# Linear attention and two feed-forward networks on one core: TensorE's order from the plan, later transfers in the plan, scalings on two engines

## The chip, the core and the metric

The kernel runs on one core of a Trainium2 chip, with TensorE (PE), VectorE (DVE), ScalarE (ACT), GpSimd (POOL) and the queue of SyncE (SP), each with its own list of instructions that it takes in order. The metric is the time of one execution on the device in us, the median of several.

## What is computed

```python
for t in range(S):                      # attention: B, H, S, D = 4, 8, 768, 64
    state = gamma * state + k[:, :, t] outer v[:, :, t]
    y[:, :, t] = scale * q[:, :, t] @ state
x = y as (3072 tokens, 512)
h = x @ w_in                            # first network, 512 -> 1024 -> 512
u = h * softmax(h)
x = ((u - mean(u)) / sqrt(var(u) + 1e-6) * g_ln) @ w_out
h = x @ w_in2                           # second network, 512 -> 2048 -> 512
out = (h * cos(h)) @ w_out2
```
(Shortened. q, k, v are float32; the weights come as 64-bit floating point numbers.)

## The kernel before

Attention runs over 24 steps: two pairs of batches, each in 12 chunks of 64 positions, all heads at once. A step loads q, k (twice: kt by dimension, kn by position) and v in six transfers, 1 MB in all. `scores` makes 16 small matmuls into bank sc, and VectorE multiplies them with the decay mask mg into X (`masks`); mg is made for each step by GpSimd from constants (`prep`), where ScalarE also scales the four parts of kn. `state` adds 16 matmuls into S, which ScalarE copies into the next step's W. `att_out` makes y, from which come xh and xl, a split of the float32 value into two parts.

Each matmul of the networks is done as three, with high and low parts (w1h, w1l and so on). In the first network `mm1` makes h of a step in bank hA (or hB for steps 1 and 3) in two halves c of 512 columns, each of 12 matmuls of 512 columns. `norm` makes u: VectorE's maximum, ScalarE's exp, VectorE's product, ScalarE's squares, GpSimd's power, and at last a scaling of u by ScalarE. Four steps make a block of 512 tokens: `transp` transposes u on TensorE into banks tr, ScalarE and VectorE make lt of it, `mm2` makes y, which ScalarE copies to ys and a transfer writes to y1d. The second network (`up`, `down`) begins when the attention is done.

The weights come in raw blocks of 512 KB. `convert` makes float32 of one: ScalarE reads the upper bits into a buffer top, VectorE joins them with the rest, and both make the high and the low part. First come eight blocks of w_in1 (tiles big, w1h, w1l), eight of w_out1 (o1h, o1l), then 32 of the second network (tiles raw), of which 28 are written back as float32 (kept) and read again later.

The order on all engines but TensorE is made at build time by `Plan.order`: each operation has an engine, an assumed duration, its dependencies and, for a transfer, an assumed landing time of LEAD + length + LAND after the issue. The plan takes the operation that can start first, at equal times the one with the longest chain behind it. TensorE's operations keep the order of the program:

```python
if at < len(pe) and need[pe[at]] == 0:
    c = [(max(free[e], ready_at[pe[at]]), pe[at])]
```
The plan's times reach the chip only as order; on the chip each instruction waits for what it needs, and all behind it on its engine wait too.

Of the kernel before, what the change touches and what calls it, by code (L numbers as in the profile page):

```python
# [24 lines left out]
C = 64  # L25
# [23 lines left out]
class Plan:  # L49
# [5 lines left out]

    SEM = 0.06
    LEAD = 1.2
    LAND = 0.6
    LANES = 8

    def __init__(self):
        self.ops = []
        self.chain = False
        self.last = []
        self.keys = []
        self.writers = {}
        self.readers = {}

    def add(self, eng, occ, fn, r=(), w=(), lat=None, port=False, xfer=0.0, after=()):
        n = len(self.ops)  # L70
        deps = {}
# [32 lines left out]
    def order(self):  # L104
# [30 lines left out]
        at = 0  # L135
# [3 lines left out]
        for i in range(n):  # L139
            if need[i] == 0 and ops[i][0] != "PE":  # L140
                pools[ops[i][0]].append(i)
        left = n
        out = []
        while left:
            best = None
            for e in free:
                if e == "PE":
                    if at < len(pe) and need[pe[at]] == 0:
                        c = [(max(free[e], ready_at[pe[at]]), pe[at])]
                    else:  # L150
                        continue
                else:
                    c = []
                    for i in pools[e]:
# [13 lines left out]
            eng, occ, fn, _, lat, prt, xfer = ops[i]  # L168
            if e == "PE":
                at += 1  # L170
            else:
                pools[e].remove(i)
# [22 lines left out]
def body(ctx: ExitStack, tc: tile.TileContext, qx, kt, kn, vn, c_sc, c_mg,  # L195
# [13 lines left out]
    mg = const.tile([128, 2, NHP, C], F32, name="mg")  # L209
    cs = const.tile([128, 3, NI, NHP], F32, name="cs")  # L210
# [38 lines left out]
    NRAW, NTOP, NWT, NA = 3, 3, 2, 3  # L249
# [20 lines left out]
    def dma(fn, size, r=(), w=(), occ=0.47, eng="SP", after=()):  # L270
# [23 lines left out]
    def load_step(n):  # L294
        bp, i = steps[n]
        s = n % NA
        X, W = a_X[s], a_W[s]
        q = qx[bp, i].rearrange("p (j s) -> p j s", s=C)
        v = vn[bp, i].rearrange("p (j s) -> p j s", s=D)
        dma(lambda: nc.sync.dma_start(out=a_kt[n % 2], in_=kt[bp, i].rearrange("p (j s) -> p j s", s=C)),  # L300
            (128, 2048), w=[("kt", n % 2)])
        dma(lambda: nc.sync.dma_start(out=X[64:128, 0], in_=q[64:128]), (64, 2048), w=[("X", s, "q", 0)], occ=0.6)
        dma(lambda: nc.sync.dma_start(out=X[0:64, 1], in_=q[0:64]), (64, 2048), w=[("X", s, "q", 1)], occ=0.6)
        dma(lambda: nc.sync.dma_start(out=a_kn[s], in_=kn[bp, i].rearrange("p (j s) -> p j s", s=2 * D)),
            (128, 2048), w=[("kn", s, a) for a in range(NHP)])
        dma(lambda: nc.sync.dma_start(out=W[0:64, 0], in_=v[0:64]), (64, 2048), w=[("W", s, "v", 0)], occ=0.6)
        dma(lambda: nc.sync.dma_start(out=W[64:128, 1], in_=v[64:128]), (64, 2048), w=[("W", s, "v", 1)], occ=0.6)
        if i == 0:
            for half, (r, par) in enumerate(((slice(64, 128), 0), (slice(0, 64), 1))):
                P.add("POOL", 0.55, lambda r=r, par=par: nc.gpsimd.memset(W[r, par], 0.0),  # L310
                      w=[("W", s, "st", half)])

    def prep(n):
# [5 lines left out]
        if i + 1 < NI:  # L319
            k = a_kn[n % NA]  # L320
            for a in range(NHP):
                act(k[:, a], k[:, a], AF.Copy, [("cs",)], [("kn", n % NA, a)], 0.295, scale=cs[:, 2, i, a:a + 1])

    def score_pair(n, j):
        k, X = a_kt[n % 2], a_X[n % NA]
        nc.tensor.matmul(out=p_sc[0:64, j], lhsT=k[64:128, j], rhs=X[64:128, 0, j], start=True, stop=True)  # L326
        nc.tensor.matmul(out=p_sc[64:128, j], lhsT=k[0:64, j], rhs=X[0:64, 1, j], start=True, stop=True)

    def state_pair(n, j):
# [3 lines left out]
        for r, par in HALF:  # L333
            nc.tensor.matmul(out=p_S[r, j], lhsT=k3[r, j], rhs=W[r, par, j],
# [595 lines left out]
```

## Time and profile before

| | us |
|---|---|
| three runs | 911.92, 914.95, 915.22 |
| profiled execution | 913.03 |
| span from its first to its last instruction | 911.3 |
| PE busy | 880.4 (97%) |
| VectorE, ScalarE, GpSimd busy | 547.6, 458.5, 45.3 |
| mean granted clock of TensorE | 0.989 |
| read and written in HBM | 64.29 and 19.92 MB, 92 GB/s over the span |

The span leaves out what lies ahead of the first and behind the last instruction. Busy shares are means over all stages. A time in a row of the timeline counts from the start of the span.

### The profile page before, as it was taken

Reading aid. Unit: us, or ns where it says so; the run is one execution under the profiler, and the core shown is the slowest. Engines: PE = TensorE matmul, PEld = TensorE weight load, DVE = VectorE, ACT = ScalarE, POOL = GpSimd, SP = SyncE. Lnnn points to the kernel's source line nnn. Section 1 sums busy time; section 2 is a strip of 40 time slices with the busy share of each in tenths; the row PEclk is TensorE's granted clock in tenths of the full one; section 3 lists DMA queues with packets and bytes.
Section 4 is the critical chain, followed back from the end, with each engine's and each line's share of the span. In section 5 each row is a group of like instructions: output and inputs, shape, how many; then the busy total and the mean of one; then the engine's idle time right before and its main releaser. Section 6 shows DMA issues by size and latency. Waiting matters only on the chain.

```text
span 911.3 us, 14625 instructions
## 1 busy us (share of the span) xinstructions
PE 880.4 (97%) x5888; PEld 725.2 (80%) x5888; DVE 547.6 (60%) x946; ACT 458.5 (50%) x768; POOL 45.3 (5%) x63
## 2 busy tenths in 40 slices
PE   5897998999999999999999999999999999999997
PEld 4686887787888878888888888888888888888886
DVE  4788756646255364746557566666665665566553
ACT  5789957766466464544334343434343443344332
POOL 2121210101011000000000000000000000000000
PEclk8998999999999999999999999999999999999999
DMA  9983599994231124130030003000200120011002
GB/s 313 286 273 93 182 295 325 299 334 148 74 105 59 47 72 149 70 116 1 1 92 1 1 1 92 1 1 24 70 0 1 45 49 1 0 30 40 1 0 47
DMA packets 38804, 85.17 MB, mean 93 GB/s; under 512 B 5456, under 2 KB 5584, under 8 KB 38736
## 3 DMA queue, kind: packets, MB, share of 16 engines
q1 hardware_dynamic: 37728, 81.80, 28.9%
q10 hardware_dynamic: 1008, 2.44, 0.8%
q8 instruction: 46, 0.75, 0.3%
q14 instruction: 22, 0.18, 0.1%
HBM read 64.29 MB, written 19.92 MB: 92 GB/s over the span
## 4 chain that ended last, share of the span: by engine, by line
PE 78%; DMA 11%; ACT 5%; DVE 4%; issue 1%; SPq 1%; POOL 0%; ACTq 0%; DVEq 0%
PE h L615 29%; PE acc L652 29%; PE hA L480 7%; PE y L546 7%; DMA raw<-w_in_dram 3%; DMA kn<-kn_dram 2%; PE tr L546 2%; DMA big<-w_in_dram 2%; PE tr L522 2%; ACT u L275 2%; DMA kept_out<-wt 1%; PE y L391 1%; ACT top L275 1%; PE sc L326 1%; DVE X L278 1%
## 5 line engine op out<-in xcount | busy, mean ns | idle before, releaser
L627 ACT ACTIVATE r<-r,hp 128x512 f32<-128x512 f32 x96 | 69.5, 724 | 146.2 <-DVE r L625 146.2
L546 PE MATMUL y<-lt,o1h 128*128 128x512 f32 x320 | 105.2, 397 | 1.3 <-ACT ys L551 1.3
L629 DVE TENSOR_TENSOR r<-r,h 128x512 f32<-128x512 f32 x96 | 66.0, 687 | 61.2 <-ACT r L627 61.2
L621 DVE SCALAR_TENSOR_TENSOR r<-ki,h 128x512 f32<-128x512 int32 x96 | 65.9, 686 | 55.3 <-ACT ki L619 55.3
L633 DVE TENSOR_TENSOR gl<-r,gh 128x512 fp32r<-128x512 f32 x96 | 66.3, 691 | 47.6 <-ACT gh L631 47.0
L652 PE MATMUL acc<-o2u,gh 128*128 128x512 f32 x288 | 94.5, 389 | 0.0
L619 ACT ACTIVATE ki<-h 128x512 int32<-128x512 f32 x96 | 57.4, 598 | 73.4 <-PE h L615 73.3
L652 PE MATMUL acc<-o2h,gh 128*128 128x512 f32 x240 | 93.4, 389 | 0.0
L652 PE MATMUL acc<-o2h,gl 128*128 128x512 f32 x240 | 93.4, 389 | 0.0
L652 PE MATMUL acc<-o2l,gh 128*128 128x512 f32 x240 | 93.4, 389 | 0.0
L631 ACT ACTIVATE gh<-r 128x512 fp32r<-128x512 f32 x96 | 60.7, 632 | 55.9 <-DVE r L629 55.9
L480 PE MATMUL hA<-w1h,xh 128*128 128x512 f32 x176 | 73.7, 419 | 3.8 <-DVE u L286 3.5
L615 PE MATMUL h<-yh,w1h 128*128 128x512 f32 x192 | 74.7, 389 | 0.0
L615 PE MATMUL h<-yh,w1l 128*128 128x512 f32 x192 | 74.7, 389 | 0.0
L615 PE MATMUL h<-yl,w1h 128*128 128x512 f32 x192 | 74.7, 389 | 0.0
L546 PEld LDWEIGHTS y<-lt,o1h 128*128 128x128 f32 x320 | 60.0, 188 | 15.3 <-ACT ys L551 1.8
L480 PE MATMUL hA<-w1h,xl 128*128 128x512 f32 x176 | 71.0, 404 | 0.0
L480 PE MATMUL hA<-w1l,xh 128*128 128x512 f32 x176 | 69.1, 398 | 0.0
L623 DVE SCALAR_TENSOR_TENSOR r<-ki,r 128x512 f32<-128x512 int32 x96 | 66.4, 692 | 3.2
L652 PEld LDWEIGHTS acc<-o2u,gh 128*128 128x128 f32 x288 | 54.1, 188 | 11.2
L546 PE MATMUL y<-lt,o1l 128*128 128x512 f32 x160 | 62.4, 390 | 0.0
L615 PE MATMUL h<-yh,w2a 128*128 128x512 f32 x192 | 59.5, 391 | 0.0
(105 smaller groups left out, 1704.8 us busy)
## 6 DMA issues: line engine op xcount, KB each, us to landing
raw<-w_in_dram SPq DMA_DIRECT2D x16, 511.8 KB, 5.9
raw<-w_out_dram SPq DMA_DIRECT2D x16, 511.8 KB, 5.4
kt<-kt_dram SPq DMA_DIRECT2D x24, 256.0 KB, 4.9
X<-qx_dram SPq DMA_DIRECT2D x48, 128.0 KB, 4.5
kn<-kn_dram SPq DMA_DIRECT2D x24, 256.0 KB, 4.7
W<-vn_dram SPq DMA_DIRECT2D x48, 128.0 KB, 4.1
y1d<-ys SPq DMA_DIRECT2D x24, 256.0 KB, 2.5
x<-y1d SPq DMA_DIRECT2D x24, 256.0 KB, 3.2
```

Source lines behind the costliest of these rows:

```text
L275: return P.add("ACT", occ, lambda: nc.scalar.activation(out=out, in_=in_, func=func, **kw), r, w, lat)
L480: nc.tensor.matmul(out=h, lhsT=a[:, k], rhs=w[:, k, s], start=(k + m == 0), stop=(k == KD - 1 and m == 2))
L546: nc.tensor.matmul(out=y1(), lhsT=w[:, j, ds], rhs=lts[j][:, a], start=(j + m == 0), stop=(j == K1 - 1 and m == 2))
L615: nc.tensor.matmul(out=p2["h2"][b], lhsT=w2tile(c, lo)[:, k, cs], rhs=p2[a][:, k], start=(k + m == 0), stop=(k == KD - 1 and m == 2))
L619: P.add("ACT", 0.5, lambda: nc.scalar.activation(out=p2["ki"][s], in_=p2["h2"][b], func=AF.Identity, scale=INV2PI, bias=0.25), [("h2", b)] ...
L621: P.add("DVE", 0.61, lambda: V.scalar_tensor_tensor(out=p2["r"][s], in0=p2["ki"][s], scalar=-C1, in1=p2["h2"][b], op0=ALU.mult, op1=ALU.ad ...
L623: P.add("DVE", 0.61, lambda: V.scalar_tensor_tensor(out=p2["r"][s], in0=p2["ki"][s], scalar=-C2, in1=p2["r"][s], op0=ALU.mult, op1=ALU.add ...
L627: P.add("ACT", 0.62, lambda: nc.scalar.activation(out=p2["r"][s], in_=p2["r"][s], func=AF.Sin, bias=hp[:, 0:1]), (), [("r", s)])
L629: P.add("DVE", 0.6, lambda: V.tensor_tensor(out=p2["r"][s], in0=p2["r"][s], in1=p2["h2"][b], op=ALU.mult), [("h2", b)], [("r", s)])
L631: P.add("ACT", 0.54, lambda: nc.scalar.activation(out=p2["gh"][g], in_=p2["r"][s], func=AF.Copy), [("r", s)], [("gh", g)])
L633: P.add("DVE", 0.6, lambda: V.tensor_tensor(out=p2["gl"][g], in0=p2["r"][s], in1=p2["gh"][g].bitcast(F32), op=ALU.subtract), [("r", s), (" ...
L652: nc.tensor.matmul(out=p2["acc"][t], lhsT=p2[a][g][:, ts_], rhs=o2tile(j, lo), start=(j == 0 and m == 0), stop=(j == K2 - 1 and m == 2))
```

## The change

`Plan.order` chooses among the next ten operations of TensorE's list: the one that can start first, where waiting for another engine costs 0.3 us more and each place in the list 0.05. A transfer is counted to land later (LAND 1.5 for 0.6, and 2.5 more for a raw weight from the ninth on, `bulk`), and a bulk transfer is placed only where the transfers ahead of it are at most 2.0 us from done. An operation may have a second form on another engine (`alt`): k's scaling and u's normalization go to ScalarE or VectorE, whichever ends first in the plan. q, k and v of a step lie in one tensor in HBM and in six slots of one tile, three tiles in turn (kt had two). The top buffers are two instead of three. The start is written anew: step 0 and the constants, now one transfer, ahead of the weights, and step 2 ahead of the last four blocks of w_in1; an exp of one column stands first on ScalarE.

```diff
-    LAND = 0.6
+    LAND = 1.5
     LANES = 8
+    BEHIND = 2.0
+    LATE = 2.5
+    WINDOW = 10
+    MARGIN = 0.3
+    STEP = 0.05
...
+        def begin(i, e):
+            occ, prt = (ops[i][1], ops[i][5]) if e == ops[i][0] else (self.alts[i][1], self.alts[i][3])
+            t = max(free[e], ready_at[i])
+            if prt and port[1] != e:
+                t = max(t, port[0])
+            if ops[i][6]:
+                t = max(t, lanes[-self.LANES])
+                if i in self.bulk:
+                    t = max(t, dma - self.BEHIND)
+            return t, occ
...
             for e in free:
                 if e == "PE":
-                    if at < len(pe) and need[pe[at]] == 0:
-                        c = [(max(free[e], ready_at[pe[at]]), pe[at])]
-                    else:
+                    c = []
+                    for k, i in enumerate(pe[:self.WINDOW]):
+                        if need[i] == 0:
+                            t = max(free[e], ready_at[i])
+                            c.append((max(free[e], ready_at[i] + self.MARGIN) + k * self.STEP, t, i))
+                    if not c:
                         continue
+                    _, t, i = min(c)
+                    if best is None or t < best[0]:
+                        best = (t, e, i)
+                    continue
...
                     for i in pools[e]:
-                        t = max(free[e], ready_at[i])
-                        if ops[i][5] and port[1] != e:
-                            t = max(t, port[0])
-                        if ops[i][6]:
-                            t = max(t, lanes[-self.LANES])
+                        t, occ = begin(i, e)
+                        if i in self.alts:
+                            t2, occ2 = begin(i, self.alts[i][0] if e == ops[i][0] else ops[i][0])
+                            if t2 + occ2 < t + occ - 1e-9:
+                                continue
...
-            eng, occ, fn, _, lat, prt, xfer = ops[i]
+            eng, occ, _, _, lat, prt, xfer = ops[i]
+            if e != eng:
+                _, occ, _, prt = self.alts[i]
+                lat = occ + 0.09
...
-                done = dma + self.LAND
+                done = dma + self.LAND + (self.LATE if i in self.bulk else 0.0)
...
+    c_all = const.tile([128, 656], F32, name="c_all")
+    mg = c_all[:, 0:512].rearrange("p (u a t) -> p u a t", u=2, t=C)
+    cs = c_all[:, 512:656].rearrange("p (u i a) -> p u i a", u=3, a=NHP)
...
-    NRAW, NTOP, NWT, NA = 3, 3, 2, 3
+    NRAW, NTOP, NWT, NA = 3, 2, 2, 3
...
-    a_kt = [pa.tile([128, 8, C], F32, name=f"kt{n}") for n in range(2)]
-    a_X = [pa.tile([128, 2, 8, C], F32, name=f"X{n}") for n in range(NA)]
-    a_kn = [pa.tile([128, NHP, 2 * D], F32, name=f"kn{n}") for n in range(NA)]
-    a_W = [pa.tile([128, 2, 8, D], F32, name=f"W{n}") for n in range(NA)]
+    a_in = [pa.tile([128, 6, 512], F32, name=f"in{n}") for n in range(NA)]
+    a_W = [[a[:, s].rearrange("p (j d) -> p j d", d=D) for s in (0, 5)] for a in a_in]
+    a_X = [[a[:, s].rearrange("p (j t) -> p j t", t=C) for s in (4, 1)] for a in a_in]
+    a_kt = [a[:, 2].rearrange("p (j t) -> p j t", t=C) for a in a_in]
+    a_kn = [a[:, 3].rearrange("p (a d) -> p a d", a=NHP) for a in a_in]
...
-        return P.add(eng, occ, fn, r, w, xfer=rows / 16 * (0.055 + row / 40000), after=after)
-    def act(out, in_, func, r, w, occ, lat=None, **kw):
-        return P.add("ACT", occ, lambda: nc.scalar.activation(out=out, in_=in_, func=func, **kw), r, w, lat)
+        return P.add(eng, occ, fn, r, w, xfer=rows / 16 * (0.032 + row / 32000), after=after, bulk=bulk)
...
+        if n == 0:
+            load(whole, (2, 3), 0, (("kt", 0), ("kt", 1)))
+            load(low, (1, 2), 3, (("q", 0),), "ACT")
+            load(high, (4, 5), 2, (("q", 1),))
+            dma(lambda: nc.scalar.dma_start(out=c_all[:, 0:656], in_=consts), (128, 2624), w=[("cs",), ("mg",)], eng="ACT")
+            load(whole, (3, 4), 1, [("kn", h) for h in range(2)])
+            weights(1)
+            load(low, (0, 1), 2, (("v", 0),))
+            load(high, (5, 6), 3, (("v", 1),))
...
-                act(k[:, a], k[:, a], AF.Copy, [("cs",)], [("kn", n % NA, a)], 0.295, scale=cs[:, 2, i, a:a + 1])
+                f = cs[:, 2, i, a:a + 1]
+                act(k[:, a], k[:, a], AF.Copy, [("cs",), ("in", n % NA, "kn", 0), ("in", n % NA, "kn", 1)], [("ks", n % NA, a)], 0.295,
+                    alt=("DVE", 0.2, lambda k=k[:, a], f=f: nc.vector.tensor_scalar(
+                        out=k, in0=k, scalar1=f, scalar2=None, op0=ALU.mult), True), scale=f)
...
-            eng="ACT" if first else "SP")
+            eng="ACT" if first else "SP", bulk=n >= K1)
...
-        act(u, u, AF.Identity, smk(8, 9), uk, 1.14, scale=sm[:, 8:9], bias=sm[:, 9:10])
+        act(u, u, AF.Identity, smk(8, 9), uk, 1.14,
+            alt=("DVE", 0.75, lambda: nc.vector.tensor_scalar(
+                out=u, in0=u, scalar1=sm[:, 8:9], scalar2=sm[:, 9:10], op0=ALU.mult, op1=ALU.add), True),
+            scale=sm[:, 8:9], bias=sm[:, 9:10])
...
     P.chained(True)
-    weights(1)
     load_to(0)
-    P.add("ACT", 0.45, lambda: nc.scalar.dma_start(out=cs, in_=c_sc.rearrange("p (u a t) -> p u a t", u=3, t=NHP)),
-          w=[("cs",)], xfer=0.56)
-    P.add("ACT", 0.45, lambda: nc.scalar.dma_start(out=mg, in_=c_mg.rearrange("p (u a t) -> p u a t", u=2, t=C)),
-          w=[("mg",)], xfer=0.85)
-    P.add("ACT", 0.45, lambda: nc.scalar.dma_start(out=gcol, in_=gln), w=[("gcol",)], xfer=0.45)
+    act(sms[2][:, 0:1], mhalf, AF.Exp, (), [("sm", 2, 0)], 1.4)
     weights(1)
     load_to(1)
-    weights(6)
+    weights(2)
+    load_to(2)
+    weights(4)
+    dma(lambda: nc.sync.dma_start(out=gcol, in_=gln), (128, 32), w=[("gcol",)])
     P.chained(False)
...
+def _steps(q, k, v):
+    q, kt, kn, v = _by_d(q, True), _by_d(k, True), _by_s(k), _by_s(v)
+    vq = np.concatenate([np.concatenate([v, q], axis=3)[:, :, :64], np.concatenate([q, v], axis=3)[:, :, 64:]], axis=2)
+    return np.ascontiguousarray(np.concatenate([kt, kn, vq], axis=3))
```

What it does to the lists of instructions, at three places. The first is SP's queue near the start, where the transfers of steps 1 and 2 and the blocks of w_in1 stand; before:
```order
L300 DMA kt_147<-kt_dram 128x512
L302 DMA X_149<-qx_dram 64x512
L303 DMA X_149<-qx_dram 64x512
L304 DMA kn_152<-kn_dram 128x512
L306 DMA W_155<-vn_dram 64x512
L307 DMA W_155<-vn_dram 64x512
L423 DMA big_111<-w_in_dram 128x2047
L423 DMA big_112<-w_in_dram 128x2047
L423 DMA big_113<-w_in_dram 128x2047
L423 DMA big_114<-w_in_dram 128x2047
L300 DMA kt_146<-kt_dram 128x512
```
The same place in the change, where in_145 is the tile of step 1, in_146 that of step 2, and big_106 to big_113 are the eight blocks:
```order
L349 DMA in_145<-qkv_dram 128x512
L349 DMA in_145<-qkv_dram 64x512 x2
L486 DMA big_108<-w_in_dram 128x2047
L486 DMA big_109<-w_in_dram 128x2047
L349 DMA in_146<-qkv_dram 128x512
L349 DMA in_146<-qkv_dram 64x512 x2
L349 DMA in_146<-qkv_dram 128x512
L349 DMA in_146<-qkv_dram 64x512 x2
L486 DMA big_110<-w_in_dram 128x2047
L486 DMA big_111<-w_in_dram 128x2047
L486 DMA big_112<-w_in_dram 128x2047
L486 DMA big_113<-w_in_dram 128x2047
```
Step 2 stood behind the last block and stands ahead of four blocks now.

The second place is TensorE's list at the first transposes, of u0 to u3, the four steps of the first block; xh1 and xl1 belong to step 5. Before:
```order
L391 MATMUL y_161<-X0_148,W0_154 64x64 x16
L522 MATMUL tr0_835<-ident_86,u0_95 128x128
L522 MATMUL tr0_835<-ident_86,u1_96 128x128
L522 MATMUL tr0_835<-ident_86,u2_97 128x128
L522 MATMUL tr0_835<-ident_86,u3_98 128x128
L522 MATMUL tr1_836<-ident_86,u0_95 128x128
```
The same place in the change:
```order
L455 MATMUL y_151<-in0_144 64x64 x16
L543 MATMUL hA_125<-w1h_89,xh1_117 128x512
L543 MATMUL hA_125<-w1h_89,xl1_119 128x512
L543 MATMUL hA_125<-w1l_90,xh1_117 128x512
L543 MATMUL hA_125<-w1h_89,xh1_117 128x512
L543 MATMUL hA_125<-w1h_89,xl1_119 128x512
L543 MATMUL hA_125<-w1l_90,xh1_117 128x512
L588 MATMUL tr0_822<-ident_85,u0_94 128x128
L588 MATMUL tr0_822<-ident_85,u1_95 128x128
L588 MATMUL tr0_822<-ident_85,u2_96 128x128
L588 MATMUL tr0_822<-ident_85,u3_97 128x128
```
Six matmuls of step 5 moved ahead of the transposes.

The third place is ScalarE's list ahead of the normalization of u3, the last row here; u4 is step 4's, in1 (before W1) the next step's state. Before:
```order
L275 ACTIVATE top2_145<-big6_113 128x512
L275 ACTIVATE kn2_153<-kn2_153,cs_79 128x128 x2
L275 ACTIVATE W1_155<-S_160 64x512
L275 ACTIVATE u4_99,sm1_83<-hA_126,sm1_83 128x1024
L275 ACTIVATE u3_98<-u3_98,sm0_82 128x1024
```
In the change:
```order
L321 ACTIVATE o1h_114<-big2_108,gcol_79 128x512
L321 ACTIVATE o1h_114<-big3_109,gcol_79 128x512
L321 ACTIVATE top0_142<-big4_110 128x512
L321 ACTIVATE u4_98,sm1_82<-hA_125,sm1_82 128x1024
L321 ACTIVATE in1_145<-S_150 64x512 x2
L321 ACTIVATE u3_97<-u3_97,sm0_81 128x1024
```
The two scalings of kn are gone from here; both copies of the state stand ahead of the normalization. Over the whole list ahead of this row ScalarE had 34 scalings of kn, 15 reads into top and the normalizations of u0 to u2; it now has 23, 13, and those of u0 and u2. Thirteen scalings and the normalization of u1 stand in VectorE's list ahead of its product of u4.

## Rows read from the trace of the kernel before

**Rows 1.** the engines by stage: stretch, its length, busy us of each engine, PE clock, DMA share, GB/s
```profile
0.00:45.80 45.80, 32.23 (x464) 25.31 (x464) 26.29 (x37) 30.11 (x59) 9.12 (x18) 0.93 0.94 299
45.80:75.00 29.20, 24.11 (x363) 19.70 (x363) 23.53 (x51) 25.82 (x46) 7.18 (x8) 0.96 0.81 247
75.00:120.00 45.00, 44.99 (x460) 37.35 (x461) 35.52 (x71) 39.63 (x73) 7.19 (x9) 0.95 0.47 144
120.00:240.00 120.00, 113.78 (x1170) 92.14 (x1169) 70.59 (x137) 79.53 (x139) 13.26 (x16) 0.99 0.81 265
395.00:912.00 517.00, 511.43 (x2257) 423.15 (x2255) 316.79 (x511) 205.12 (x328) 0.00 (x0) 1.00 0.10 27
```

**Rows 2.** waits of the PE, 0 to 46 us: who waits for whom, total, times, longest
```profile
PE sc L326 <- DMA X<-qx_dram: 6.8, 1, 6.8
PE S L334 <- DMA W<-vn_dram: 1.9, 1, 1.9
PE hA L480 <- DVE u L286: 1.6, 1, 1.6
```

**Rows 3.** waits of the PE, 46 to 120 us
```profile
PE tr L522 <- ACT u L275: 5.1, 1, 5.1
```

**Rows 4.** waits of the PE, 120 to 400 us
```profile
PE tr L522 <- DVE lt L533: 4.1, 3, 2.3
PE hA L480 <- DVE u L286: 1.9, 2, 1.1
PE y L546 <- ACT ys L551: 1.3, 1, 1.3
```

**Rows 5.** timeline of the PE: start, duration (us), instruction, idle time ahead of it
```profile
41.98 0.27 PE L326 MATMUL sc<-X,kt 64*64 64x64 f32 x1
75.01 1.33 PE L522 MATMUL tr<-ident,u 128*128 128x128 f32 x5 [5.09 <-ACT u L275]
76.56 0.63 PE L480 MATMUL hA<-w1h,xl 128*128 128x512 f32 x1
76.98 0.63 PE L480 MATMUL hA<-w1l,xh 128*128 128x512 f32 x1
```

**Rows 6.** the engines by stage again, three early stretches
```profile
0.00:12.00 12.00, 4.06 (x63) 3.72 (x64) 3.12 (x4) 3.89 (x7) 5.67 (x15) 1.00 0.84 257
12.00:25.40 13.40, 11.19 (x142) 8.28 (x140) 8.73 (x14) 11.03 (x20) 1.04 (x1) 0.75 1.03 356
46.00:50.00 4.00, 4.00 (x18) 3.29 (x18) 3.97 (x13) 3.20 (x7) 1.05 (x1) 1.00 1.05 341
```

**Rows 7.** the page's part 6, DMA issues: count, size, median us to landing
```profile
raw<-w_in_dram SPq DMA_DIRECT2D x16, 511.8 KB, 5.9
kt<-kt_dram SPq DMA_DIRECT2D x24, 256.0 KB, 4.9
```

**Rows 8.** timeline of ScalarE (ACT)
```profile
28.90 2.19 ACT L275 ACTIVATE kn<-kn,cs 128x128 f32<-128x128 f32 x7
69.43 2.01 ACT L275 ACTIVATE top<-big 128x512 f16<-128x512 bf16 x3
73.72 1.23 ACT L275 ACTIVATE u<-u,sm 128x1024 f32<-128x1024 f32 x1
```

**Rows 9.** one line of VectorE: min, median and max ns
```profile
L625 DVE TENSOR_SCALAR r<-r x96: 418/426/428, 365.4 to 897.7; 128x512 f32<-128x512 f32 x96
```

**Rows 10.** groups of VectorE, 0 to 120 us: count, busy us, mean ns, idle before
```profile
L282 DVE TENSOR_SCALAR sm<-sm 128x1 f32<-128x1 f32 x16 | 1.9, 148 | 0.0
```

**Rows 11.** timeline of VectorE, the same operation twice
```profile
8.11 1.19 DVE L286 SCALAR_TENSOR_TENSOR big<-big,top 128x512 int32<-128x512 int32 x1 [8.11 <-ACT top L275]
13.79 0.69 DVE L286 SCALAR_TENSOR_TENSOR big<-big,top 128x512 int32<-128x512 int32 x1 [1.72 <-ACT top L275]
```

**Rows 12.** waits of ScalarE, 120 to 240 us
```profile
ACT top L275 <- DMA raw<-w_out_dram: 12.0, 9, 2.9
ACT top L275 <- DMA raw<-w_in_dram: 10.9, 7, 3.2
```

More of the change, by code (lines that the diff above doesn't have):

```diff
@@ L67, in __init__, with add @@
         self.readers = {}
-    def add(self, eng, occ, fn, r=(), w=(), lat=None, port=False, xfer=0.0, after=()):
+    def add(self, eng, occ, fn, r=(), w=(), lat=None, port=False, xfer=0.0, after=(), alt=None, bulk=False):
         n = len(self.ops)
+        if alt:
+            self.alts[n] = alt
+        if bulk:
+            self.bulk.add(n)
         deps = {}
@@ L122, in order @@
             eng, occ, _, _, lat, _, xfer = ops[i]
+            if i in self.alts and self.alts[i][1] < occ:
+                lat -= occ - self.alts[i][1]
+                occ = self.alts[i][1]
             tail = lat + self.SEM + (self.LEAD + xfer + self.LAND if xfer else 0)
@@ L138, in order, with ready @@
         lanes = [0.0] * self.LANES
-        for i in range(n):
+        def ready(i):
             if need[i] == 0 and ops[i][0] != "PE":
                 pools[ops[i][0]].append(i)
+                if i in self.alts:
+                    pools[self.alts[i][0]].append(i)
+        def begin(i, e):
[8 more added lines that the diff above has]
+            return t, occ
+        for i in range(n):
+            ready(i)
         left = n
@@ L184, in order @@
                 ready_at[s] = max(ready_at[s], done if full else t)
-                if need[s] == 0 and ops[s][0] != "PE":
-                    pools[ops[s][0]].append(s)
-            out.append(i)
+                ready(s)
+            out.append(self.alts[i][2] if e != eng else ops[i][2])
             left -= 1
@@ L304, in load_step, with load @@
[L304 to L307, printed above, removed]
+        W = a_W[s]
+        def load(r, slots, col, w, eng="SP"):
+            e = nc.scalar if eng == "ACT" else nc.sync
+            c = slots[1] - slots[0]
+            dma(lambda: e.dma_start(out=a_in[s][r, slots[0]:slots[1]],
+                                    in_=qkv[bp, i, r, col * 512:(col + c) * 512].rearrange("p (c f) -> p c f", f=512)),
+                (r.stop - r.start, c * 2048), w=[("in", s, *x) for x in w], occ=0.47 if r.stop - r.start == 128 else 0.6, eng=eng)
@@ new lines, in load_step @@
+        whole, low, high = slice(0, 128), slice(0, 64), slice(64, 128)
+        if n == 0:
[7 more added lines that the diff above has]
+            load(high, (5, 6), 3, (("v", 1),))
+        else:
+            load(whole, (2, 3), 0, (("kt", 0), ("kt", 1)))
+            load(low, (1, 2), 3, (("q", 0),))
+            load(high, (4, 5), 2, (("q", 1),))
+            load(whole, (3, 4), 1, (("kn", 0), ("kn", 1)))
+            load(low, (0, 1), 2, (("v", 0),))
+            load(high, (5, 6), 3, (("v", 1),))
@@ L338, in k_sc @@
         s = n % NA
-        return [("kt", n % 2), ("X", s, "q", 0), ("X", s, "q", 1)], [("sc",)]
+        return [("in", s, x, h) for x in ("kt", "q") for h in (0, 1)], [("sc",)]
     def k_S(n):
         s = n % NA
-        return [("kn", s, a) for a in range(NHP)] + [("W", s, "v", 0), ("W", s, "v", 1)], [("S",)]
+        return [("in", s, x, h) for x in ("kn", "v") for h in (0, 1)] + [("ks", s, a) for a in range(NHP)], [("S",)]
     def scores(n):
@@ L739, in attend @@
         if n == ns - 1:
[L740 removed]
+            p2["sb_hook"] = [P.add("HOOK", 0.0, open_sb, lat=0.0, after=P.using({"in", "amg", "sc", "S", "y"}))]
     def first(n, c):
@@ L862, in body @@
             down(NBLK - 1, j, [t])
-    for i in P.order():
-        P.ops[i][2]()
+    for fn in P.order():
+        fn()
 _OUTS = [((NT, DM), "float32")]
```

63 lines of the change are left out of this document (28 added, 35 removed).

## The prediction

> **What bounds the kernel now.** I read the time of each engine by stage first. From 395 us on the PE is busy 511.43 of 517 us [rows 1] with 2257 instructions, 0.227 us each, at a granted clock of 1.00; what is missing there is the tail behind the last matmul. Nothing that orders the work better can win time in that half. Ahead of it the PE is idle for 13.6 us up to 45.8, 5.1 us up to 75, none up to 120, and 6.2 us up to 240. So the whole gain to be had lies ahead of 395 us, nearly all of it ahead of 240.
>
> Then the PE's waits, stretch by stretch. In the first 46 us it waits 6.8 us for the first q transfer, 1.9 us for a v transfer and 1.6 us for bank hA, which VectorE has to leave first [rows 2]. Up to 120 us one wait counts: the first transposes stand 5.1 us for ScalarE's normalization of u [rows 3]. Later come three waits for VectorE's lt, two for its u and one for ScalarE's ys, 7.3 us in all [rows 4].
>
> The timeline shows what such a wait costs beyond itself. The transposes go on at 75.01, and behind them two matmuls start 0.42 us apart [rows 5], against the 0.227 us above: the lower of the clock's two levels, 1.2 instead of 2.4 GHz, after 5.1 idle us. The same shows early: 0.75 granted on the mean between 12 and 25.4 us [rows 6].
>
> **The start, up to the first joint scores and state, 41.98 us now [rows 5].** The transfers bind here: 1.03 of the DMA engines' time at 356 GB/s between 12 and 25.4 us, 257 GB/s before [rows 6]. So arrival is set by the order of bytes. The change puts step 0 (1 MB) and the constants (0.34 MB) ahead of the first raw weight, joins the two constant transfers, and sends one q half from ScalarE's queue, where a 512 KB weight went first. A kt transfer takes 4.9 us at the median to land [rows 7], so the first matmul can't come before 4.9 us and comes at 6.8 now; I take 5.7, 1.1 us won.
>
> Behind that, three steps, the constants and the eight w_in1 blocks are 7.3 MB. By the two rates 3.1 MB are in at 12 us and 7.9 MB at 25.4 us, so all is there at 24 us, converted some 3 us later. Step 2 (1 MB, 3 us at that rate) has moved ahead of the last four blocks; that delays the second halves of step 0 and 1, and the new PE order fills in with the first halves. The PE's own work up to the mark is 32.23 us [rows 1] less the 2.2 us between 41.98 and the 1.6 us wait that ends at 45.8, so 30.0; from 5.7 without a gap that ends at 35.7. At the full clock the 11.19 us of 12 to 25.4 would be 8.4, so 32.9 is the lower bound. If only the first matmul moves, the mark is at 40.9. I take 34.5, nearer the bound, since each wait listed there is for something that now arrives earlier: **7.5 us** (1.1 to 9.1).
>
> On the q half from the second queue the Trainium skill, DMA: Bandwidth & Descriptors, section "Issuing engines are not separate DMA queues", speaks against: transfers of all engines share the same 16 DMA engines, and a second issuer saves its issue time only. By it the 1.1 us must come from the weight that steps back and not from the queue; were that not so, the start would keep its 6.8 and the total would be 1.1 us higher. No row of this trace separates the two.
>
> **From there to the first transposes.** ScalarE is busy 25.82 of 29.2 us in this stage and VectorE 23.53 [rows 1], and both take their queues in order. ScalarE's list ahead of u3's normalization loses 11 of 34 scalings of k (2.19 us for seven [rows 8], so 3.4), two of 15 top reads (2.01 for three, 1.3) and one u normalization (1.2): 5.9 us. That alone lets it end at 69.1 instead of 75.0; started earlier by part of the 7.5, I put it at 67.5, so the 7.5 us are carried and not added to. If ScalarE's start doesn't move with the PE's, 2 us are left of them; if the wait goes away, 3 us more come in.
>
> Of the fifth step's matmuls six now stand ahead of the transposes: 6 x 0.227 = **1.4 us** of work in the wait. They need bank hA, free after VectorE has u4, and that comes behind ScalarE's exp of u4 which also stands ahead of u3's normalization; so they fit. The two parts of the wait are shorter than 5.1, and after the 1.6 us wait that ends at 45.8 the clock stayed at 1.00 [rows 6]. The half clock costs 8 x 0.2 = 1.6 us now; I take half, **0.8 us** (0 to 1.6).
>
> VectorE takes over these operations. Its scaling of 128x128 and normalization of 128x1024 don't occur in the trace; 426 ns for 128x512 [rows 9] and 148 ns for one column [rows 10] give 0.54 ns a column, so estimates of 0.22 and 0.70 us. Thirteen scalings and one normalization ahead of u4's product make 3.6 us on an engine with 5.7 idle us in the stage. Beside GpSimd's mg product a VectorE operation of 0.69 us took 1.19 [rows 11]; for the 8 mg products of this stage 0 to 4.0 us. Most of it hides behind the idle time: I take **-0.5 us**. Fewer top buffers (three to two) cost nothing while ScalarE's reads of top's source are a read apart from VectorE's use; without that cover a read waits for one VectorE operation, 0.7 us.
>
> **120 to 395 us.** ScalarE waits here 12.0 and 10.9 us for raw weights [rows 12], and what the PE waits for (lt, u, ys) is queued behind these reads. The old plan lets a raw block land 3.1 us after its issue (1.2 + 1.3 + 0.6), the new one 6.5 with its extra 2.5; the median for a raw block of w_in is 5.9, and for kt the plan goes from 2.7 to 3.5 against 4.9 [rows 7]. So the new order puts the reads where the data is nearer to being there. It doesn't make a transfer faster, and SP's queue still carries as many. Of the 6.2 us up to 240 I take half, **3.1 us** (0 to 6.2). The last 1.1 us wait, for u at the end of the first network, gets six second-layer matmuls (1.4 us) put ahead of it: **1.1 us**.
>
> The six slots as such cost and win nothing: six transfers a step before and after, of the same bytes. The second network keeps its order, but for half an up block ahead of the first down block.
>
> **Sum.** 7.5 + 1.4 + 0.8 - 0.5 + 3.1 + 1.1 = 13.4 us. The profiled execution took 913.0 us (span 911.3), so 899.6, told as 900. The median shown is 914.95, 1.9 us above that execution. From no change a measurement of this kernel tells about 0.5%, 4.6 us.
>
> **Rivals.** *The gain goes further:* the mark at 32.9, the half clock (1.6) and 3 us of the wait gone, all of 7.3 us later: 9.1 + 1.4 + 1.6 + 3 + 7.3 = 22.4, 891. For it: the idle time is there [rows 1]. Against: ScalarE has only 3.4 idle us in the stage.
>
> *The start is eaten at the transposes:* ScalarE has the same list between the exp of u3 and its normalization, and what the PE wins it waits away. 2 + 1.4 - 0.5 + 3.1 + 1.1 = 7.1, 906. For it: 25.82 of 29.2 us busy.
>
> *It does nothing that counts:* step 2's 1 MB ahead of the last weights takes 3 us, the mark stays, and the reads on ScalarE still wait as before. Only 1.4 and 1.1 are left: 910.5.
>
> *VectorE becomes the bound, and it gets slower:* 3.6 us of new work and 4.0 us of meetings with GpSimd ahead of u4, none of it in VectorE's idle time because that idle time lies ahead of operations that wait for ScalarE in order. 913.0 + 7.6 - 1.4 = 919. It decides if over 4 of the 7.6 us stay uncovered. For it: 1.19 instead of 0.69 us [rows 11]; against: 5.7 idle us, and ScalarE's list gets shorter by more. The Trainium skill, SBUF — State Buffer, section "Who interferes with whom", states such a rule: VectorE and GpSimd share one pair of ports under an exclusive lock, for VectorE's tensor_scalar in its two-port mode as for operations with two SBUF inputs, while ScalarE waits for nobody. The one row agrees (0.50 us more), and by the rule the scalings would have been safer on ScalarE.
>
> **Chances.** 0.47 for the forecast, 0.15 further, 0.20 eaten, 0.10 nothing, 0.08 VectorE. Faster by over 0.5% (below 910.4) are the first three, 0.82; 0.10 same; 0.08 slower. 889 to 910 takes in the forecast's own range (893 to 905), the eaten start and nearly all of the further one, 0.8.
>
> **What would show it.** The first matmul near 5.7; the first joint scores and state near 34.5; the first transposes' wait split by six matmuls, going on at 66 to 67, with less than 2 us at half clock behind; ScalarE's waits for raw weights between 120 and 240 well under 22.9 us; from the first down block on the same 0.227 us. I am wrong if the first joint scores and state stay near 41, if the transposes wait for VectorE, or if a wait for a weight transfer stands in the PE's new order.

## The result, and the profile after

Median 900.62 us of four runs (899.51 to 902.04) against 915.09 of four of the kernel before (911.92 to 917.07): ratio 0.9846, interval 0.9812 to 0.9880. The profiled execution took 899.53 us against 913.03, 13.5 us less; the forecast was 900.0 and 13.4. The sum came out; its terms did not, so the sum came out by luck, as the last sections show.

The engines by stage in the changed kernel, columns as in [rows 1]:

```profile
0.00:45.80 45.80, 32.72 (x481) 26.51 (x482) 30.46 (x50) 26.73 (x51) 9.25 (x18) 1.00 0.94 282
45.80:75.00 29.20, 24.18 (x360) 19.91 (x359) 25.37 (x56) 26.25 (x45) 6.54 (x7) 0.88 0.89 284
75.00:120.00 45.00, 45.00 (x467) 37.11 (x467) 35.47 (x75) 32.27 (x58) 7.91 (x9) 1.00 0.52 167
120.00:240.00 120.00, 120.00 (x1299) 99.58 (x1298) 86.35 (x175) 67.69 (x114) 14.43 (x17) 1.00 0.81 265
```

The third number is the PE's busy time: from 75 to 240 us it is never idle; up to 75 it still is, for 18.1 us, nearly as long as before (18.7). Its waits, the longest in each of the stretches of [rows 2 to 4]:

```profile
PE sc L390 <- DMA in<-qkv_dram: 5.9, 2, 5.4
PE S L398 <- DMA in<-qkv_dram: 2.8, 1, 2.8
PE hA L543 <- ACT w1h L321: 2.0, 2, 1.8
PE hA L543 <- DVE u L332: 1.9, 1, 1.9
...
PE hA L543 <- DVE u L332: 5.0, 1, 5.0
...
PE y L612 <- ACT ys L617: 0.7, 1, 0.7
```

To see where time was won, the same work must be compared. The matmuls of attention's y come once a step; steps count from 0. Their first rows for steps 4, 7, 10 and 16 in the timeline of the PE, before:

```profile
52.56 0.63 PE L391 MATMUL y<-X,W 128*64 128x64 f32 x14
85.33 0.86 PE L391 MATMUL y<-X,W 128*64 128x64 f32 x22
127.05 1.15 PE L391 MATMUL y<-X,W 128*64 128x64 f32 x32
221.16 1.03 PE L391 MATMUL y<-X,W 128*64 128x64 f32 x28
```

and in the changed kernel:

```profile
48.66 0.86 PE L455 MATMUL y<-in 128*64 128x64 f32 x22
81.23 0.98 PE L455 MATMUL y<-in 128*64 128x64 f32 x26
123.14 1.03 PE L455 MATMUL y<-in 128*64 128x64 f32 x28
207.49 0.69 PE L455 MATMUL y<-in 128*64 128x64 f32 x16
```

The differences of the starts are the lead: 3.9 us at step 4 (ahead of the first transposes), 4.1 at step 7 (behind them), 3.9 at step 10, 13.7 at step 16. Ahead of each of these four rows TensorE has done the same number of matmuls of every kind in both kernels, and in every other kernel below, so the leads compare equal work. So 9.8 of 13.5 us come between 127 and 221 us (times of the kernel before), where 3.1 were forecast and 6.2 taken as the most. What changed there is on ScalarE. Its waits from 120 to 240 us, the largest and those for raw weights:

```profile
ACT u L321 <- DVE sm L561: 18.3, 7, 3.9
ACT ys L617 <- PE y L612: 12.4, 5, 6.3
...
ACT top L321 <- DMA raw<-w_out_dram: 2.2, 1, 2.2
```

For raw weights it waited 22.9 us before [rows 12], 2.2 now. It waits longer for VectorE and for TensorE, but TensorE itself has no wait in this stretch, so that costs nothing. How such reads cost TensorE time shows in ScalarE's timeline before (start, duration, instruction, idle time ahead): three stalls for raw weights of 3.0 us together, one of 1.94 us for VectorE's x, and at the end of the list the row that makes lt from transposes that TensorE began at 133.73:

```profile
126.53 0.79 ACT L275 ACTIVATE top<-raw 128x512 f16<-128x512 bf16 x1 [1.24 <-DMA raw<-w_out_dram]
128.57 0.79 ACT L275 ACTIVATE top<-raw 128x512 f16<-128x512 bf16 x1 [1.24 <-DMA raw<-w_out_dram]
...
132.16 0.79 ACT L275 ACTIVATE top<-raw 128x512 f16<-128x512 bf16 x1 [0.50 <-DMA raw<-w_out_dram]
134.89 0.64 ACT L275 ACTIVATE xh<-x 128x512 fp32r<-128x512 f32 x1 [1.94 <-DVE x L278]
...
137.94 0.60 ACT L551 ACTIVATE ys<-y 128x512 f32<-128x512 f32 x1
138.43 1.08 ACT L531 ACTIVATE lt<-tr 128x512 fp32r<-128x512 f32 x2
```

VectorE's joins wait for the same reads (0.94 us at 127.36, behind the first of them), so a late transfer delays both lists. In the changed kernel the same transposes begin at 129.82:

```profile
128.45 0.78 ACT L321 ACTIVATE top<-raw 128x512 f16<-128x512 bf16 x1
130.02 0.60 ACT L617 ACTIVATE ys<-y 128x512 f32<-128x512 f32 x1 [0.79 <-PE y L612]
130.51 1.08 ACT L597 ACTIVATE lt<-tr 128x512 fp32r<-128x512 f32 x2
```

lt follows 0.7 us behind the start of its transposes instead of 4.7, and ScalarE (0.79 us for y) waits for TensorE, no longer the other way round.

### The profile page after: what moved, and what is told of

The parts are those of the page before. It is cut to its first block, busy times and chain, and to the rows that moved or that the text cites. A ratio compares the mean times of both kernels' runs of the same rounds, so it can differ in the third digit from the quotient of the medians.

```text
span 897.7 us, 14593 instructions
## 1 busy us (share of the span) xinstructions
PE 873.6 (97%) x5888; PEld 722.6 (80%) x5888; DVE 571.2 (64%) x1014; ACT 421.5 (47%) x701; POOL 45.9 (5%) x62
## 4 chain that ended last, share of the span: by engine, by line
PE 90%; DMA 4%; DVE 2%; ACT 2%; issue 0%; SPq 0%; ACTq 0%
PE h L681 29%; PE acc L718 29%; PE y L612 12%; PE hA L543 11%; DMA in<-qkv_dram 4%; PE tr L612 2%; PE tr L588 2%; PE y L455 2%; PE sc L390 1%; DMA big<-w_in_dram 1%; ACT junk L321 1%; ACT u L321 0%; DVE in L324 0%; DVE u L332 0%; DVE sm L561 0%; PE S L398 0%
## 5 line engine op out<-in xcount | busy, mean ns | idle before, releaser
L543 PE MATMUL hA<-w1h,xl 128*128 128x512 f32 x176 | 69.0, 392 | 0.0
```

The costliest lines, as they stand in the source:

```text
L543: nc.tensor.matmul(out=h, lhsT=a[:, k], rhs=w[:, k, s], start=(k + m == 0), stop=(k == KD - 1 and m == 2))
```

## The experiments

Theory L: the later landing time in the plan won the 9.8 us, because ScalarE no longer stands before raw weights with lt, ys or u queued behind. Rivals: A, ScalarE's shorter list did it; W, TensorE's choice of order did. Each median is compared with that of the kernel before on its own chip. "Lead" is against the one profile of before (913.03 us), as above; "raw" is ScalarE's wait for raw weights from 120 to 240 us. A lead comes from one profile each, while six executions of the changed kernel lie between 899.54 and 903.50 us. So a difference of 1 to 4 us between two rows up to step 10 may be that of the execution and not of the kernel; what is won between steps 10 and 16, 9.6 to 9.8 us in some rows and -1.5 to 1.2 in the others, is far beyond that.

| kernel | median us | ratio, 95% interval | lead at step 4, 7, 10, 16 | raw |
|---|---|---|---|---|
| changed | 900.62 | 0.9846 (0.9812 to 0.9880) | 3.9, 4.1, 3.9, 13.7 | 2.2 |
| changed, again | 902.86 | 0.9844 (0.9815 to 0.9874) | 0.8, 4.1, 3.9, 13.7 | 1.5 |
| old_land | 915.57 | 1.0018 (0.9990 to 1.0046) | -1.1, 2.9, -4.0, -2.9 | 28.7 |
| no_alt | 903.01 | 0.9873 (0.9822 to 0.9924) | -0.5, 3.3, -0.6, 9.0 | 1.9 |
| fixed_pe | 904.02 | 0.9877 (0.9838 to 0.9916) | -0.7, 0.3, -0.6, 9.2 | 4.6 |
| old_start | 900.21 | 0.9836 (0.9796 to 0.9876) | -0.4, 2.6, 2.4, 12.2 | 4.7 |
| b_land | 904.62 | 0.9865 (0.9833 to 0.9896) | -1.1, 0.0, 0.0, 9.5 | 3.1 |
| no_bulk | 911.02 | 0.9923 (0.9893 to 0.9953) | 1.7, -0.5, -1.5, -0.5 | 33.6 |
| no_late | 912.94 | 0.9959 (0.9932 to 0.9987) | 3.9, 3.3, 2.0, 0.5 | 26.9 |
| no_behind | 899.50 | 0.9814 (0.9778 to 0.9850) | 0.6, 2.2, 2.0, 11.7 | 3.9 |
| late5 | 899.48 | 0.9811 (0.9777 to 0.9845) | 2.6, 7.8, 6.9, 16.7 | 0.3 |
| o1_late2 | 898.86 | 0.9809 (0.9778 to 0.9840) | 0.2, 5.9, 4.6, 14.4 | 4.8 |
| late5_o1 | 899.08 | 0.9801 (0.9769 to 0.9834) | 0.9, 4.3, 4.3, 14.1 | 0 |

**old_land**, the old landing time in the changed kernel:

```diff
-    LAND = 1.5
-    BEHIND = 2.0
-    LATE = 2.5
+    LAND = 0.6
+    BEHIND = 1e9
+    LATE = 0.0
```

> The changed kernel with the old landing allowance (LAND 0.6, no LATE, no BEHIND); all else as changed. At equal work the changed kernel won 9.8 us between 127 and 221 us of the old one, where no wait of TensorE is left. Theory L (the later landing did it, as ScalarE no longer stands before raw weights with lt and u behind it): the waits come back, 7 to 10 us slower, 908 to 911, ScalarE again waits over 15 us for raw blocks between 120 and 240 us, the first 120 us within 1 us. Theory A (ScalarE's shorter list did it): within 2 us of 900.6, the waits for raw blocks are back but nobody on TensorE stands. Theory W (TensorE's choice of order fills the waits): within 2 us too, with another order of TensorE around the transposes.

The whole gain is gone. ScalarE's waits from 120 to 240 us, and two of the PE's from 100 to 240:

```profile
ACT top L321 <- DMA raw<-w_out_dram: 15.5, 10, 2.8
ACT top L321 <- DMA raw<-w_in_dram: 13.2, 7, 2.8
```
```profile
PE tr L588 <- DVE lt L599: 3.7, 1, 3.7
PE y L612 <- ACT ys L617: 3.1, 1, 3.1
```

The waits are back for lt and ys, as theory L has it: of the 9.8 us between steps 10 and 16, 1.2 are left. It is slower than expected since the stretch up to step 10 loses 7.9 us against the changed kernel too, where 1 at most was expected; 6.0 of them come between steps 9 and 10, where the wait for ys and matmuls at half clock behind it lie.

**no_alt**, both scalings on ScalarE alone (the `alt` of k's scaling and of u's normalization taken out):

```diff
-                    alt=("DVE", 0.2, lambda k=k[:, a], f=f: nc.vector.tensor_scalar(
...
-            alt=("DVE", 0.75, lambda: nc.vector.tensor_scalar(
```

> The changed kernel with k's scaling and u's normalization on ScalarE alone; all else as changed. Theory L (later landing won the 9.8 us between 127 and 221 us): 1 to 3 us slower at most, from the first 80 us. Theory A (ScalarE's shorter list did it): 7 to 12 us slower, 908 to 913, with waits of TensorE for ScalarE's u or for lt between 120 and 240 us. For the first transposes: VectorE's product of u4 started late behind two joins and four scalings of k (2.2 us); if the scalings matter there, the wait of 5.0 us shrinks by about 1; if ScalarE's list is as tight as before, it grows by up to 3.

Between steps 10 and 16 it wins 9.6 us, with ScalarE's full list, so rival A falls. At the first transposes TensorE waits 1.9 us instead of 5.0, for ScalarE's normalization. Against the changed kernel it is behind by 4.5 us at step 10 already; 3.9 of them come after step 9, at one wait of the PE and the half clock behind it:

```profile
PE y L607 <- ACT ys L612: 1.9, 1, 1.9
```

**fixed_pe**, TensorE in program order:

```diff
-    WINDOW = 10
+    WINDOW = 1
```

> The changed kernel with TensorE in program order (WINDOW 1); all else as changed. Theory W (the choice of order fills the waits): 6 to 12 us slower, most of it before 45 us and around 130 to 220 us. Theory L and A: between 120 and 395 us within 1 us of the changed kernel; at the first transposes no loss, since the six matmuls put ahead of them stood 5.0 us for VectorE themselves; at the start 1 to 3 us slower, 901.5 to 904.

9.8 us between steps 10 and 16: rival W falls as well. But at step 7 the lead is 0.3 instead of 4.1. So up to there, contrary to what was expected, TensorE's choice of order was worth something, or the lists that the plan makes for the other engines along with it; the run can't tell these apart. Its waits from 46 to 120 us:

```profile
PE tr L588 <- DVE u L574: 3.5, 1, 3.5
PE hA L543 <- DVE u L332: 3.0, 3, 1.6
```

**old_start**, the old order of loads at the start (the block of weights inside step 0 is taken out too):

```diff
     P.chained(True)
+    weights(1)
     load_to(0)
...
     load_to(1)
-    weights(2)
-    load_to(2)
-    weights(4)
+    weights(6)
```

> The changed kernel with the loads at the start in the old order (one weight block, step 0, constants, one block, step 1, six blocks; step 2 behind them); all else as changed. If the order of loads won the 3.9 us that the changed kernel is ahead at the mark of 45 us: 3 to 5 us slower there, 904 to 906 in all. If TensorE's new order won them and the loads nothing: within 1 us of 900.6. If the lead is eaten at the first transposes (5.0 us for VectorE's u4): later at 45 us by 3 to 5 but at 80 us within 1 us.

The lead at step 4 is gone (-0.4) and more than half of it is back at step 7 (2.6); the time is the changed kernel's within what can be measured. So what the loads win by step 4 is mostly eaten at the transposes. How much they win by step 4 is open, since the changed kernel itself has 3.9 in one profile and 0.8 in the other. The first matmul, start and wait:

```profile
8.03 0.33 PE L389 MATMUL sc<-in 64*64 64x64 f32 x1 [8.03 <-DMA in<-qkv_dram]
```

Half of q still comes from ScalarE's queue here, behind a weight again, and the first matmul comes at 8.03 us instead of 5.45 (6.83 in the kernel before). So the second queue alone did not win the 1.4 us at the first matmul; the order was needed. Whether the order alone would do, with all of q on SP's queue, was not run. The Trainium skill, DMA: Bandwidth & Descriptors, section "Issuing engines are not separate DMA queues", says that transfers of all issuers run on the same 16 DMA engines. The run agrees: with the weight ahead, the second queue brought q no earlier.

**b_land**, the kernel before with the landing time alone:

```diff
-    LAND = 0.6
+    LAND = 1.5
+    BEHIND = 2.0
+    LATE = 2.5
...
+                            if i in self.bulk:
+                                t = max(t, dma - self.BEHIND)
...
-                done = dma + self.LAND
+                done = dma + self.LAND + (self.LATE if i in self.bulk else 0.0)
```

> The kernel before with the landing allowance of the change alone (LAND 1.5; LATE 2.5 and BEHIND 2.0 for raw weights from the ninth); TensorE in program order, scalings on ScalarE, old start. Theory L (the later landing alone clears TensorE's waits between 127 and 221 us): 8 to 10 us faster than before, 903.5 to 905.5, ScalarE's waits for raw blocks between 120 and 240 us fall from 22.9 to under 6 us, and the lead at 120 us is within 1.5 us of nothing. Rival J (it needs the shorter list of ScalarE or TensorE's choice with it): under 4 us faster, waits of TensorE for lt or ys stay.

As theory L expected: nothing won up to 127 us, 9.6 between 127 and 221, with the old lists of TensorE and the old scalings. By the ratios the constants alone give 1.35% of the 1.54%, by the profiles 9.5 of 13.7 us at step 16. The engines by stage:

```profile
75.00:120.00 45.00, 45.00 (x459) 37.28 (x458) 35.69 (x70) 41.10 (x77) 7.18 (x9) 0.94 0.54 170
120.00:240.00 120.00, 119.63 (x1210) 98.72 (x1209) 71.88 (x137) 79.35 (x139) 13.83 (x16) 1.00 0.80 259
```

**no_bulk**, **no_late**, **no_behind**: which of the three constants. The edits are LATE 0.0 and BEHIND 1e9; LATE 0.0 alone; BEHIND 1e9 alone.

> The changed kernel without the extra allowance for raw weights (LATE 0, BEHIND off), LAND 1.5 kept. By the measured landing (median 6.1 us for a raw block; planned 4.0 to 4.2 by LAND 1.5, 6.5 to 6.7 with LATE): if the reads of raw blocks still come before their data, 4 to 8 us slower than 900.6, ScalarE's waits for raw blocks between 120 and 240 us at 10 to 20 us. If LAND alone does it: within 1.5 us, waits under 5 us.

> The changed kernel with LATE 0 and BEHIND 2.0 kept (LAND 1.5). Without both the 9.8 us between 127 and 221 us fell to 1.0. Theory P (the planned landing time, so the place of the reads in ScalarE's list, wins them): as without both, 1 to 3 us won in that stretch, ScalarE's waits for raw blocks over 12 us, 905 to 911 in all. Theory B (BEHIND, which holds a raw transfer back until the queue ahead is short, wins them): 8 us or more won in the stretch, waits under 5 us, 900 to 903.

> The changed kernel with LATE 2.5 kept and BEHIND off. Theory P (the planned landing time): 8 us or more won between 127 and 221 us, ScalarE's waits for raw blocks under 8 us, 899 to 903 in all. Theory B (BEHIND): under 3 us won there, waits over 12 us, 905 to 911.

Between steps 10 and 16 they win 1.0, -1.5 and 9.8 us. LATE does it and BEHIND doesn't matter; whether LATE would do it with the old LAND of 0.6 was not run. Without LATE the loss was larger than expected: 33.6 us of waits for raw weights in no_bulk, where 10 to 20 were expected, and 912.94 us for no_late, where 905 to 911 were. LAND 1.5 alone plans a raw block 4.0 us after its issue (1.2 + 1.3 + 1.5), and its data come later: the medians in no_late are

```profile
raw<-w_in_dram SPq DMA_DIRECT2D x16, 511.8 KB, 5.8
raw<-w_out_dram SPq DMA_DIRECT2D x16, 511.8 KB, 5.5
```

**late5**, an allowance beyond the measured landing:

```diff
-    LATE = 2.5
+    LATE = 5.0
```

> The changed kernel with LATE 5.0 for 2.5: raw weights planned to land 9.2 us after the issue, about 3 us later than the median. If an allowance beyond the measured landing costs nothing: within 1 us of 900.6 and no wait of TensorE between 120 and 240 us. If it makes the weights late, since a buffer is held longer: 2 to 6 us slower, with waits of TensorE or of SP's queue for raw buffers in that stretch, or a later first step of the second network.

It plans the data 9.0 us after the issue (median 5.4 and 5.2 in this run) and costs nothing: 9.8 us between steps 10 and 16 again. Its profile has 3.7 us more lead at step 7, and not from raw waits. LATE also counts for the blocks of w_out1: at step 7 ScalarE has made o1h of five of them, instead of all eight, and eight transposes stand ahead of step 5's matmuls, as in o1_late2 below. That one of these won the 3.7 us is not shown.

**o1_late2**, to find what holds the first transposes:

```diff
-    def convert(src, use, first=False):
+    def convert(src, use, first=False, gate=()):
...
-                (o1h[:, j], o1l[:, j], ("o1h", j), ("o1l", j), gcol[:, j:j + 1]))
+                (o1h[:, j], o1l[:, j], ("o1h", j), ("o1l", j), gcol[:, j:j + 1]),
+                gate=[("u", 3, 0)] if j >= 2 else ())
```

(`gate` is one more input of the read into top; the later blocks are put behind step 4 in the program.)

> The changed kernel with the conversion of the blocks 2 to 7 of w_out1 planned behind u3's normalization. It tests what holds the first transposes (wait of 5.0 us for VectorE's product of u4). Theory Q (the lists of VectorE and ScalarE are full there, the conversions stand ahead): two joins and two subtractions of 0.7 us less on VectorE ahead of the product, so the wait shrinks by 1.5 to 3 us, and with it the 1.4 us at half clock may go: 896.5 to 899.5, if the conversions don't come late for the second layer. Rival D (the wait is for data, the chain of maximum, exp and product behind hA's last matmul, not for the list): wait within 0.7 us of 5.0, and 900 or slower by a new wait for o1h or o1l.

The lead goes from 0.2 at step 4 to 5.9 at step 7. This is left of the 5.0 us wait, in the timeline of the PE:

```profile
69.19 1.36 PE L589 MATMUL tr<-ident,u 128*128 128x128 f32 x8
71.77 0.50 PE L544 MATMUL hA<-w1h,xh 128*128 128x512 f32 x1 [1.22 <-DVE u L332]
```

Theory Q holds in part. The wait is shorter (1.22 us, against 5.02 and 2.63 in two profiles of the changed kernel) and no half clock follows. But eight transposes now stand ahead of it, since u3's normalization, on VectorE here, comes earlier: the edit changed TensorE's order too. And rival D does not fall: from the start of VectorE's maximum to the matmul of hA it takes 4.7 us here (67.12 to 71.77) and 4.8 in both profiles of the changed kernel (65.80 to 70.55, 66.47 to 71.23, below). What the conversions can delay is the start of the maximum.

**late5_o1** joins the two last edits, and **after2** is the changed kernel again, on the same chip.

> The changed kernel with LATE 5.0 and with the blocks 2 to 7 of w_out1 converted behind u3's normalization. Each alone made the first transposes come earlier at equal work (3.7 and 1.8 us) by taking work from ahead of u4's product. If they take away the same wait: as LATE 5.0 alone, within 1.5 us of it, 895 to 898 in a profile. If they add: 892 to 895. If the conversions now collide with the second layer: 899 or more.

> The changed kernel once more, to compare on one chip: 898 to 902.

They don't add: a lead of 4.3 at step 7, less than either alone. By the medians late5_o1 is 3.8 us (0.4%) faster than the changed kernel beside it; five of six executions of the changed kernel are slower than all six of late5_o1, yet the intervals of the two ratios overlap, so that it is faster is likely and not certain. The second profile of the changed kernel is the more useful result. In its timelines the PE has a wait of 1.6 us for X that the first doesn't have, and half clock behind the next wait:

```profile
39.16 0.27 PE L390 MATMUL sc<-in 64*64 64x64 f32 x1 [1.59 <-DVE in L324]
43.40 0.63 PE L543 MATMUL hA<-w1h,xh 128*128 128x512 f32 x1 [1.90 <-DVE u L332]
...
66.05 0.39 PE L543 MATMUL hA<-w1l,xh 128*128 128x512 f32 x1
...
71.23 0.80 PE L543 MATMUL hA<-w1h,xh 128*128 128x512 f32 x1 [2.63 <-DVE u L332]
```
```profile
66.47 1.23 DVE L561 TENSOR_REDUCE sm<-hA 128x1 f32<-128x1024 f32 x1
```

The lead at step 4 is 0.8 instead of 3.9, and at step 7 it is 4.1 as in the first. The wait at the transposes is 2.63 instead of 5.02 and TensorE goes on at 71.23 instead of 70.55: its lead ahead of them hardly counts. Here VectorE's maximum starts as soon as the last matmul of hA (66.05) has ended, so the list ahead of it costs nothing, and 2.63 us of wait are left all the same.

## Why the prediction was right in sum and wrong in its parts

Of its signs, the first matmul (5.45 us), the waits for raw weights (2.2 us) and the 0.227 us a matmul behind 395 us came true. The first joint scores and state, the split wait and the short half clock did not, and one sign of being wrong came true: TensorE waits for VectorE at the transposes. That the time is right all the same is luck: terms that were too large and one that was too small cancelled.

**The start, 7.5 us.** The first matmul came at 5.45 us (forecast 5.7), the first joint scores and state at 37.67, and at 39.16 in the second profile (forecast 34.5): 4.3 and 2.8 us won, inside the bounds of 1.1 to 9.1 but far below the value taken. The price was put near the bound of a TensorE that never waits; it still waited 1.8 us for w1h from ScalarE and 2.8 for v. (The 7.3 MB there are 7.7 million bytes, in the unit of the rates; at these rates all is there at 24.9 us, not 24. No term hangs on it.)

**"So the 7.5 us are carried and not added to".** This step failed. The lead at step 7 is 4.1 us whether it was 3.9 or 0.8 at step 4, and with the loads of old it rises from -0.4 to 2.6. VectorE sets the time there: in both profiles TensorE goes on 4.8 us behind the start of its maximum. The rival "the start is eaten at the transposes" named the mechanism; it had the engine wrong. Its 2 us have no working: by ScalarE's shorter list alone, 5.9 would be left.

**Six matmuls ahead of the transposes, 1.4 us, and half of the half clock, 0.8 us.** Both failed. The six went ahead as the order shows, but waited themselves:

```profile
70.55 0.79 PE L543 MATMUL hA<-w1h,xh 128*128 128x512 f32 x1 [5.02 <-DVE u L332]
71.14 0.63 PE L543 MATMUL hA<-w1h,xl 128*128 128x512 f32 x1
71.57 0.63 PE L543 MATMUL hA<-w1l,xh 128*128 128x512 f32 x1
...
73.28 1.90 PE L588 MATMUL tr<-ident,u 128*128 128x128 f32 x8
```

The wait was not split: the prediction had said that bank hA is free in time because u4's product comes before u3's normalization. So it does, but the product itself comes late. The prediction had a price for what is new on VectorE ahead of it (3.6 us, hidden but for 0.5), none for the time from hA's last matmul to the product. That matmul of step 4 starts at 62.97; VectorE then does this:

```profile
63.81 1.29 DVE L332 SCALAR_TENSOR_TENSOR big<-big,top 128x512 int32<-128x512 int32 x2
65.01 0.87 DVE L385 TENSOR_SCALAR in<-in,c_all 128x128 f32<-128x128 f32 x4
65.80 1.21 DVE L561 TENSOR_REDUCE sm<-hA 128x1 f32<-128x1024 f32 x1
...
69.27 1.22 DVE L332 SCALAR_TENSOR_TENSOR u<-u,hA 128x1024 f32<-128x1024 f32 x1
```

Two joins and four scalings of k stand ahead of the maximum, 2.0 us. From its start to 70.55 it takes 4.8 us more: the maximum, ScalarE's exp, the product and what stands between them. Matmuls at the lower clock, 0.43 us apart, go on up to 75.2, about as long as before. The granted clock is 0.88 against 0.96 from 45.8 to 75 us, and 1.00 against 0.95 from 75 to 120: the half clock came earlier, it did not get shorter.

**VectorE and ScalarE share the scalings, -0.5 us.** No loss showed, and the one run points the other way: without the sharing the kernel has 4.7 us less lead at step 16 in its one profile, 3.9 of them by the wait for ys ahead of step 10. By the ratios it wins 0.27% less, but the intervals overlap, so the sign stays open. VectorE's scaling took 0.22 us in a row of four and its normalization 0.81 (estimates 0.22 and 0.70). Of the 8 operations of GpSimd in the stage 45.8 to 75 us four are mg products, so the meetings of the prediction come to 0 to 2.0 us and not to 4.0, and its rival of a bound on VectorE to 917 instead of 919. That rival fell with the time, though the wait at the transposes did become VectorE's.

**120 to 240 us, 3.1 us (0 to 6.2).** The mechanism was right: later places for the reads of raw weights. Its size and its bound were wrong; 9.6 to 9.8 us were won there in all ten profiles with LATE 2.5 or 5.0, and 1.2, 1.0 and -1.5 in the three with LATE 0. The bound counted the idle time, 6.2 us. A wait costs more: by the leads at the rows of the timeline, the wait of 0.79 us at 163.9 gave 1.1 back, that of 1.33 at 181.6 gave 1.6, that of 1.58 at 216.2 gave 2.0. These are 0.3 to 0.4 us each on top. The wait of 2.30 us at 139.8 had eight matmuls 0.43 us apart behind it, 1.6 us more than at full clock. 6.2 + 1.6 leave 2.0 of the 9.8 for the five waits, 0.4 each. And the half that was taken had no row behind it: 22.9 us of waits for raw weights, with lt and ys queued behind them and VectorE's list waiting for the same reads, spoke for all of it.

**The wait at 336 us, 1.1 us.** 0.4 us: the wait for u went, and one of 0.7 us for ys came in its place.

**Sum by stages.** 4.1 up to step 7 (forecast 9.2 with the six matmuls, the clock and VectorE's part), -0.2 up to step 10, 9.8 up to step 16, 0.4 at the end of the first network, -0.5 behind TensorE's last matmul (5.3 us to the end of the span instead of 4.8): 13.6 from span to span. Two errors of about 5 and 7 us cancelled. What stays open is the share of each part up to 75 us: fixed_pe, old_start and no_alt lose 3.8, 1.5 and 0.8 us of the 4.1 at step 7, which don't add, late5 won 3.7 there by other lists, and each is one profile.

## What to carry to other kernels

Where instructions are ordered by a plan and taken in order, a read of a transfer should be planned at the time its data are measured to land, or later: too early stalls all that is queued behind it, too late cost nothing here up to 3.6 us beyond the median (late5: 9.0 planned, 5.4 measured). What a stall of TensorE is worth is its idle time, plus 0.3 to 0.4 us here, plus the matmuls at half clock behind it. And a lead won ahead of a wait is only worth something if the engines waited for have won it too.

## What the hardware showed that was not expected

The executions of one kernel differ in the first 70 us: behind a wait of 1.9 us the clock went to its lower level at 43.40 us in one profile of the changed kernel (matmuls 0.43 us apart) and stayed up in the other. With the wait of 1.6 us for X, 3.1 us of lead were gone at step 4, to come back at the transposes.

A scaling of k of 128x128 on VectorE takes 0.22 us in a row; three that met GpSimd's mg took 1.46 us. The first of them, 1.07 us long, ended 0.07 us behind mg; the other two took their usual time. The mg itself took 1.48 us instead of 1.05; a join of VectorE was under way when it began:

```profile
199.72 1.46 DVE L385 TENSOR_SCALAR in<-in,c_all 128x128 f32<-128x128 f32 x3
```
```profile
199.23 1.48 POOL L377 TENSOR_TENSOR mg<-c_all 128x512 f32<-128x512 f32 x1 [11.87 <-DVE sm L328]
```

TensorE had no wait there, so it cost nothing. The Trainium skill, SBUF — State Buffer, section "Who interferes with whom", says that VectorE's tensor_scalar can contend with GpSimd for ports that one of them holds alone for a whole instruction; the rows agree.
